# Score tiles of a windowed attention grouped by key tile instead of query tile, in a fused attention and gMLP kernel

## The chip, the cores and the metric

The kernel runs on one core of one Trainium2 chip. The metric is device time in microseconds (us) of one launch, as the median of several runs.

## The reference

Four batches, eight heads, 768 positions, head size 64. Attention keeps the first 4 keys (sinks) and the last 128 positions (the window); a gated MLP with a mixing matrix over positions follows.

```python
scores = q @ k.T / sqrt(64)
keep = (key < 4) | ((0 <= query - key) & (query - key < 128))
a = softmax(where(keep, scores, -1e9))
x = (a @ v) with the heads side by side            # 4 x 768 x 512
h = gelu_tanh(x @ w_in)                            # 512 -> 1024
u, v = h[..., :512], h[..., 512:]
v_n = (v - mean(v)) / sqrt(var(v) + 1e-6) * g_ln
v_s = w_sg @ v_n + b_sg                            # mixes the 768 positions
out = x + (u * v_s) @ w_out
```

## The kernel before, in words

Positions are cut into six tiles of 128. With a window of 128 a query tile i needs only two key tiles, i (the causal triangle) and i-1 (the other triangle), and the four sinks. Heads are taken in pairs p = 0 to 3: the two heads of a pair lie in the lower and the upper 64 rows, so their score matmuls use one half of TensorE's rows each.

The whole kernel is one list of steps, STEPS, written out by hand. The program walks it once, and each engine gets its instructions in that order, one queue for each engine. A step is a name, indices and sometimes a letter for the engine (D VectorE, A ScalarE, P GpSimd). Nothing is reordered afterwards: an instruction that waits holds back all that stands behind it on its engine. The steps that matter here, with batch b, pair p and group g:

- LQ.b.t, LK.b.t (line 223) load one 128-position tile of q or k in bf16. They are issued by GpSimd and share one queue with the loads of v (LVH) and of the weights (LW, LWS, LWO).
- TQ.b.g, TK.b.g transpose two tiles, 2g and 2g+1, of q or k on TensorE (line 377) into a slot of the mm ring; EQ.b.g and EK.b.g copy the result out (lines 197, 198). In batch 0 a step takes a pair of heads and all six tiles (line 371). In batch 3 DQ.3.g and DK.3.g do it by DMA on SyncE's queue (SP) instead.
- QK.b.p.g (lines 473 and 478) makes the score tile of group g, for both heads of the pair, in a slot of the sc ring. In some steps of batch 0 a mask is added first by a matmul with the identity (line 473).
- EX.b.p.g (line 483) is the exponential into a tile P[b, p, g]; MK.b.p.g masks it, by a multiplication on VectorE (line 490) or by two selects on GpSimd (lines 493 and 496).
- SK.b.g (line 457) and SX.b.g (line 462) make the scores of the sinks and their exponential.
- AV.b.p.k (lines 519, 523 and 526) multiplies with v: for each query tile the diagonal part, the part of the previous key tile, and the sinks. In batch 0 one step makes two query tiles, in the others three. NR.b.p.k divides by the sum (lines 535 and 536) into x_sb.
- XT, XE or XD.b.h (a DMA transpose on SP) transpose x_sb into xT; MV (line 561) and GV (line 565), MU (line 602) and GU (line 607) are the first matmul and the Gelu; BN, RS, NM and Z the normalization; SP.b.h.dc (line 622) the mixing matmul, GT (line 627) and GM (line 632) the gate; OU.b.t (line 639), RA.b.t (line 643) and ST.b.t the last matmul, the addition and the store. (The step SP has nothing to do with the engine SP.)
- Steps of one batch are interleaved with those of the next: the attention of batch 1 and 2 runs beside the MLP of the batch before it.

Memory is held in rings: a step that makes a tile takes the next slot and has to wait until all readers of the tile that was there are done. The sc ring has 2 slots, the mm ring 4 (shared by TQ, TK, SK, AV, XT, SP, OU), the P ring 10.

A score tile of group g in the kernel before has 512 columns for each head (384 for g=0), grouped by the two query tiles 2g and 2g+1: key 2g with queries 2g and 2g+1 in columns 0 to 255, key 2g+1 with query 2g+1 in 256 to 383, and, for g>0, key 2g-1 with query 2g in 384 to 511.

Of the kernel before, what the change touches and what calls it, by code (L numbers as in the profile page):

```python
# [28 lines left out]
XE.0.1.A LK.1.2 NR.0.0.2 MK.0.3.2.D LK.1.3 NR.0.1.2 AV.0.2.2 AV.0.3.2 LQ.1.2 NR.0.2.2 GV.0.0 MV.0.1 NR.0.3.2 LQ.1.3  # L29
BN.0.0 LWS.1 XT.0.2 GV.0.1 MU.0.1 XE.0.2.A BN.0.1 WT.0 GU.0.1 TK.1.0 MV.0.2 RS.0.1 EK.1.0.A LK.1.4 NM.0.1 WE.0.A WT.1  # L30
GV.0.2 LK.1.5 TK.1.1 MU.0.2 LB.P EK.1.1.A BN.0.2 Z.0.0.A LK.2.0 WT.2 GU.0.2 MU.0.0 WE.1.D RS.0.2 WE.2.D Z.0.1.A LQ.2.0
NM.0.2 Z.0.2.A Z.0.3.D Z.0.4.D WT.3 LQ.2.1 WT.4 GU.0.0 WE.3.D WT.5 LQ.1.4 Z.0.5.D TQ.1.1 QK.1.0.0 EQ.1.1.D QK.1.1.0
LQ.1.5 SP.0.0.0 WE.4.D LK.2.1 EX.1.0.0 VSM.1 SP.0.0.1 WE.5.D EX.1.1.0 LVH.1.0 GT.0.0.0 TK.1.2 KS.1 GT.0.0.1 QK.1.2.0
QK.1.3.0 EX.1.2.0 SP.0.0.2 LVH.1.1 GM.0.0.0.D EX.1.3.0 MK.1.2.0.D TQ.2.0 EK.1.2.A LQ.2.2 QK.1.0.1 EQ.2.0.D QK.1.1.1
TQ.1.2 EX.1.0.1 GT.0.0.2 LWO SP.0.0.3 EQ.1.2.D EX.1.1.1 LK.2.2 MK.1.0.1.D TK.2.0 MK.1.0.0.D QK.1.2.1 LK.2.3 EK.2.0.A
QK.1.3.1 MK.1.3.0.D SK.1.0 GM.0.0.1.D LQ.2.3 SP.0.1.0 EX.1.2.1 GT.0.0.3 MK.1.1.0.D LQ.2.4 EX.1.3.1 SP.0.1.1 MK.1.1.1.D
LQ.2.5 MK.1.2.1.D SX.1.0 QK.1.0.2 QK.1.1.2 GT.0.1.0 EX.1.0.2 GM.0.0.2.P SP.0.1.2 GT.0.1.1 EX.1.1.2 LK.2.4 GM.0.1.0.D
AV.1.0.0 MK.1.3.1.D AV.1.1.0 LK.2.5 GM.0.0.3.D QK.1.2.2 GT.0.1.2 QK.1.3.2 EX.1.2.2 SP.0.1.3 NR.1.0.0 MK.1.1.2.P
EX.1.3.2 NR.1.1.0 AV.1.2.0 AV.1.3.0 MK.1.0.2.P GT.0.1.3 QK.2.0.0 QK.2.1.0 NR.1.2.0 EX.2.0.0 OU.0.0 MK.1.2.2.P NR.1.3.0
TK.2.1 RA.0.0 AV.1.0.1 XD.1.0 EK.2.1.A MK.1.3.2.P AV.1.1.1 NR.1.0.1 AV.1.2.1 EX.2.1.0 GM.0.1.2.P NR.1.1.1 AV.1.3.1  # L40
NR.1.2.1 QK.2.2.0 LK.3.0 QK.2.3.0 EX.2.2.0 OU.0.1 NR.1.3.1 GM.0.1.3.P EX.2.3.0 OU.0.2 XD.1.1 RA.0.1 GM.0.1.1.P TK.2.2
MK.2.3.0.D TQ.2.1 LVH.2.0 TQ.2.2 EQ.2.1.D MV.1.0 EQ.2.2.D LQ.3.0 EK.2.2.D LQ.3.1 VSM.2 MU.1.0 GV.1.0 MK.2.1.0.D
# [33 lines left out]
def kernel(  # L76
# [14 lines left out]
    nc = tc.nc  # L91
# [9 lines left out]
    NT = S // 128  # L101
# [326 lines left out]
    def at(ring, b):  # L428
        if HOW[b] in "AGL":
            return ring[b].rearrange("p (c t i) -> p t c i", c=HP, t=NT)  # L430
        return ring[b].rearrange("p (t c i) -> p t c i", c=HP, t=NT)
# [31 lines left out]
                             func=AF.Exp, scale=scale)  # L463

    def wide(g):
        return 512 if g else 384

    def QK(b, p, g, biased=0):
        sc = fresh(sc_ring, (b, p, g))
        w = wide(g)  # L470
        if biased:
            for hl in range(2):
                nc.tensor.matmul(sc[:, hl, 0:w], iden, (bias1 if g else bias0)[:, 0:w], start=True, stop=False)
        pieces = [(2 * g, 2 * g, 2, 0), (2 * g + 1, 2 * g + 1, 1, 256)] + ([(2 * g - 1, 2 * g, 1, 384)] if g else [])
        for n, (j, i, ni, c) in enumerate(pieces):
            for hl in range(2):
                rows = slice(64 * hl, 64 * hl + 64)
                nc.tensor.matmul(sc[:, hl, c:c + 128 * ni], at(kT, b)[rows, j, p, :], at(qT, b)[rows, i:i + ni, p, :],  # L478
                                 start=not biased, stop=(not biased or n == len(pieces) - 1))

    def EX(b, p, g):
        w = wide(g)
        nc.scalar.activation(out=P.new((b, p, g))[:, :, 0:w], in_=sc_ring[b, p, g][:, :, 0:w], func=AF.Exp, scale=scale)  # L483

    def MK(b, p, g, e="D"):
        w = wide(g)
        pt = P[b, p, g]
        if e == "D":
            m = (mask1 if g else mask0)[:, 0:w]
            nc.vector.tensor_mul(pt[:, :, 0:w], pt[:, :, 0:w], m.unsqueeze(1).to_broadcast([128, 2, w]))  # L490
            return
        p4 = pt.rearrange("p h (j i) -> p h j i", i=256)
        nc.gpsimd.affine_select(out=p4[:, :, :, 0:128], in_=p4[:, :, :, 0:128], compare_op=ALU.is_ge,  # L493
                                fill=0.0, base=0, pattern=[[0, 2], [0, 2], [1, 128]],
                                channel_multiplier=-1)
        nc.gpsimd.affine_select(out=p4[:, :, :, 128:256], in_=p4[:, :, :, 128:256],
                                compare_op=ALU.is_ge, fill=0.0, base=-1,
                                pattern=[[0, 2], [0, 2], [-1, 128]], channel_multiplier=1)

    def rowsof(b, k):  # L500
        return (2 * k, 2) if b in PARTS else (3 * k, 3)

    def av_view(b, p, k):
        n = rowsof(b, k)[1]
        return mm_ring["a", b, p, k][:, 0:2 * n * (Dh + 1)].rearrange("p (i h d) -> p i h d", i=n, h=2)

    def AV(b, p, k):
        vb = v_sb[b]
        fresh(mm_ring, ("a", b, p, k))
        av = av_view(b, p, k)  # L510
        i0, n = rowsof(b, k)
        first = True
        for il in range(n):
            i = i0 + il
            for hl in range(2):
                h = 2 * p + hl
                pt = P[b, p, i // 2]
                c = 256 * (i % 2)
                nc.tensor.matmul(av[:, il, hl, :], pt[:, hl, c:c + 128], vb[:, h, i, :], start=first, stop=False)  # L519
# [191 lines left out]
```

## Time and profile before

| | |
|---|---|
| median of 3 runs | 156.57 us (156.06 to 156.64) |
| profiled execution: span, first to last instruction | 155.8 us |
| TensorE matmul, busy | 147.2 us (94%), 1543 instructions |
| VectorE, busy | 123.0 us (79%) |
| GpSimd, busy | 99.7 us (64%) |
| ScalarE, busy | 98.9 us (63%) |
| score matmuls, line 478 | 256 instructions |
| software DMA queue (loads issued by GpSimd) | 64608 packets, 11.01 MB, 97.1% of 16 engines' span |

The profile is of one execution, with its own span of 155.8 us; no other time of that execution is given, and the median of the runs is 0.77 us above the span. In the profile PE is TensorE's matmuls, PEld its weight loads, DVE is VectorE, ACT ScalarE, POOL GpSimd, SP SyncE. A row of a group gives line, engine and operation, what is written and read, the count, the busy time and the mean of one in ns, and the idle time of the engine ahead of it with what ended it. A row of the chain or of the timeline begins with the start and the duration in us. A row of a stretch gives its length, the busy time and count of PE, PEld, DVE, ACT and POOL, the granted TensorE clock (1.00 is full), and the DMA share and rate.

### The profile page before, as it was taken

What the parts mean: (1) busy time and instruction counts of PE and PEld (TensorE: products, weight loads), DVE (VectorE), ACT (ScalarE), POOL (GpSimd) and SP (SyncE); (2) the same over time, 40 slices, a digit from 0 to 9 for tenths busy, and PEclk for the clock granted to TensorE, in tenths of its full rate; (3) what the DMA queues carried; (4) which work ended last, traced back from release to release, by engine and by line L of the source; (5) the groups of instructions that cost most, each with busy time, mean ns of one, the idle gap of its engine ahead of it and who ended that gap; (6) DMA issues with size and microseconds to landing.
All of it is one profiled execution on the core that took longest, in us unless ns stands there. A gap on an engine that the chain in (4) does not pass through costs nothing.

```text
span 155.8 us, 3844 instructions
## 1 busy us (share of the span) xinstructions
PE 147.2 (94%) x1543; PEld 95.0 (61%) x1543; DVE 123.0 (79%) x295; ACT 98.9 (63%) x110; POOL 99.7 (64%) x127
## 2 busy tenths in 40 slices
PE   6998799999999999989999999999999999999990
PEld 2455487779775776747566764486567644876530
DVE  4576688829989989769789887899689956867981
ACT  3689789799989856276897855269954025591000
POOL 4099669578999899999559869640798610300400
PEclk9999689999999999999999999999999999999999
DMA  5899999999999999999999299995710580510064
GB/s 162 277 369 155 152 194 163 170 186 200 141 144 145 188 157 169 148 152 156 155 227 235 68 279 177 181 192 47 248 72 6 99 236 0 202 64 9 0 230 176
DMA packets 86170, 24.67 MB, mean 158 GB/s; under 512 B 78660, under 2 KB 83016, under 8 KB 86152
## 3 DMA queue, kind: packets, MB, share of 16 engines
q0 software_dynamic: 64608, 11.01, 97.1%
q1 hardware_dynamic: 21544, 13.41, 32.1%
q8 instruction: 12, 0.20, 0.5%
q14 instruction: 6, 0.05, 0.1%
HBM read 24.81 MB, written 6.29 MB: 200 GB/s over the span
## 4 chain that ended last, share of the span: by engine, by line
PE 75%; DMA 15%; DVE 2%; POOL 2%; issue 1%; ACT 1%; SPq 1%; ACTq 0%
PE mm L622 17%; PE sc L561 13%; PE mm L639 13%; PE sc L602 12%; DMA k<-in_k_dram 6%; DMA v_sb<-in_v_dram 6%; PE sc L478 5%; PE mm L519 4%; DMA uT<-in_k_dram 4%; PE mm L377 3%; PE mm L523 3%; PE mm L526 2%; PE mm L614 1%; PE mm L545 1%; DVE P L490 1%
## 5 line engine op out<-in xcount | busy, mean ns | idle before, releaser
L483 ACT ACTIVATE P<-sc 128x1024 bf16<-128x1024 f32 (+1 forms) x48 | 43.5, 956 | 10.9 <-PE sc L478 10.8
L622 PE MATMUL mm<-wsgT,z 128*128 128x384 bf16 x192 | 34.1, 327 | 0.0
L622 PEld LDWEIGHTS <-z 128*128 128x128 bf16 x192 | 17.7, 98 | 11.9 <-issue 0.7
L561 PE MATMUL sc<-w_in_sb,xT 128*128 128x512 bf16 x96 | 22.2, 379 | 0.7 <-ACT vt L565 0.7
L639 PE MATMUL mm<-w_out_sb,wsg_gated 128*128 128x512 bf16 x96 | 22.7, 379 | 0.0
L493 POOL TENSOR_SCALAR_AFFINE_SELECT P<-P 128x512 bf16<-128x512 bf16 x21 | 14.0, 665 | 13.3 <-ACT P L483 13.0
L627 DVE SCALAR_TENSOR_TENSOR gtmp<-mm,g_sb,b_bc 128x384 bf16<-128x384 f32 x32 | 19.1, 610 | 4.2 <-PE mm L622 3.6
L602 PE MATMUL sc<-xT,w_in_sb 128*128 128x256 bf16 x192 | 22.1, 273 | 0.0
L632 POOL TENSOR_TENSOR wsg_gated<-gtmp,uT 128x384 bf16<-128x384 bf16 x15 | 14.9, 1005 | 10.9 <-DVE gtmp L627 10.9
L574 DVE BATCH_NORM_STATS2 st<-vt 128x6 f32<-128x512 f32 x24 | 15.4, 684 | 7.5 <-ACT vt L565 7.4
L602 PEld LDWEIGHTS <-w_in_sb 128*128 128x128 bf16 x192 | 18.7, 98 | 3.0
L536 DVE TENSOR_TENSOR x_sb<-mm,rcp 128x384 bf16<-128x384 f32 (+1 forms) x36 | 18.5, 513 | 1.2
L565 ACT ACTIVATE vt<-sc 128x1024 f32<-128x1024 f32 x12 | 12.3, 1027 | 9.0 <-PE sc L561 8.9
L519 PE MATMUL mm<-v_sb,P 128*128 128x65 bf16 x192 | 16.8, 198 | 1.0 <-DMA v_sb<-in_v_dram 0.9
L643 DVE TENSOR_TENSOR ot<-mm,x_sb 128x512 f32<-128x512 f32 x24 | 16.1, 683 | 2.0 <-PE mm L639 1.9
L583 POOL TENSOR_TENSOR rs<-rs,neg_half 128x4 f32<-128x4 f32 (+1 forms) x8 | 7.0, 869 | 16.4 <-DVE rs L578 15.0
L519 PEld LDWEIGHTS <-P 128*128 128x128 bf16 x192 | 15.1, 100 | 2.9 <-issue 1.5
L223 POOL DMA_DIRECT2D q<-in_q_dram x18 | 16.7, 949 | 0.0
L223 POOL DMA_DIRECT2D k<-in_k_dram x18 | 16.4, 924 | 0.5 <-POOL wsg_gated L632 0.5
L523 PE MATMUL mm<-v_sb,P 128*128 128x65 bf16 x160 | 16.1, 197 | 0.0
L561 PEld LDWEIGHTS <-xT 128*128 128x128 bf16 x96 | 9.2, 98 | 10.9 <-issue 0.9
L478 PE MATMUL sc<-qT,kT 64*128 64x128 bf16 (+1 forms) x256 | 15.1, 242 | 0.6 <-ACT P L483 0.3
(90 smaller groups left out, 238.0 us busy)
## 6 DMA issues: line engine op xcount, KB each, us to landing
out_dram<-ot SPq DMA_DIRECT2D x24, 256.0 KB, 2.3
v_sb<-in_v_dram POOLq DMA_DIRECT2D x8, 384.0 KB, 8.5
q<-in_q_dram POOLq DMA_DIRECT2D x18, 128.0 KB, 6.3
k<-in_k_dram POOLq DMA_DIRECT2D x18, 128.0 KB, 6.5
wsg_gated<-in_moe_w_sg_dram POOLq DMA_DIRECT2D x2, 576.0 KB, 7.5
w_in_sb<-in_moe_w_in_dram POOLq DMA_DIRECT2D x2, 512.0 KB, 10.1
uT<-in_q_dram SPq DMA_DIRECT2D x2, 384.0 KB, 3.1
uT<-in_k_dram SPq DMA_DIRECT2D x2, 384.0 KB
```

The costliest lines, as they stand in the source:

```text
L223: return nc.gpsimd.dma_start(out=dst.rearrange("p (h d) -> p h d", h=H), in_=heads(src, b, i))
L478: nc.tensor.matmul(sc[:, hl, c:c + 128 * ni], at(kT, b)[rows, j, p, :], at(qT, b)[rows, i:i + ni, p, :], start=not biased, stop=(not biase ...
L483: nc.scalar.activation(out=P.new((b, p, g))[:, :, 0:w], in_=sc_ring[b, p, g][:, :, 0:w], func=AF.Exp, scale=scale)
L519: nc.tensor.matmul(av[:, il, hl, :], pt[:, hl, c:c + 128], vb[:, h, i, :], start=first, stop=False)
L523: nc.tensor.matmul(av[:, il, hl, :], pt[:, hl, c:c + 128], vb[:, h, i - 1, :], start=False, stop=(i < 2 and il == n - 1 and hl == 1))
L536: nc.vector.tensor_mul(x_sb.get(b)[:, i0:i0 + n, 128 * p:128 * (p + 1)].rearrange("p t (h d) -> p t h d", h=2), av[:, :, :, 0:Dh], rcp[:, ...
L561: nc.tensor.matmul(hp[:, jl, :], xT[b][:, 2 * g + jl, c, :], w_in_sb[:, c, d_half:2 * d_half], start=(c == 0), stop=(c == KD - 1))
L602: nc.tensor.matmul(hp[:, dc // 2, 256 * (dc % 2):256 * (dc % 2 + 1)], w_in_sb[:, c, 128 * dc:128 * (dc + 1)], xT[b][:, 2 * g:2 * g + 2, c, :],
L622: nc.tensor.matmul(ps[:, 0:NH], z[b][:, si, 128 * dc:128 * (dc + 1)], wsgT[:, si, NH * hf:NH * (hf + 1)], start=(si == 0), stop=(si == NT ...
L627: nc.vector.scalar_tensor_tensor(out=gtmp.new((b, hf, dc)), in0=mm_ring["g", b, hf, dc][:, 0:NH], scalar=g_sb[:, dc:dc + 1], in1=b_bc[:, N ...
L639: nc.tensor.matmul(ps, gated(b, hf)[:, dc, 128 * tl:128 * (tl + 1)], w_out_sb[:, dc, :], start=(dc == 0), stop=(dc == KU - 1))
L643: nc.vector.tensor_add(ot.new((b, t)), mm_ring["o", b, t], x_sb[b][:, t, :])
```

## The change

The score tiles are grouped by key tile. The tile of group g now holds key 2g with queries 2g and 2g+1, and key 2g+1 with queries 2g+1 and 2g+2, 256 columns each; the last group (g=2) has only query 5 for key 5, so it is the one with 384 columns. A step has two matmuls per head instead of three (g=0 had two already). AV takes the part of the previous key tile from the tile of the group that this key belongs to. The second select on GpSimd covers one block per head instead of two in the last group.

Since QK.b.p.g now reads query tile 2g+2, some steps move: EQ.1.1 ahead of QK.1.0.0 (which now stands behind SP.0.0.0), TQ.1.2 and EQ.1.2 ahead of QK.1.0.1 in exchange for TQ.2.0 and EQ.2.0, and TQ.2.1 and EQ.2.1 from behind TK.2.2 to behind SP.0.1.3 and NR.1.0.0, ahead of QK.2.0.0. The loads keep their order. In STEPS, lines 32 to 42 change (only moved steps and their neighbours are shown, the line breaks are not):

```diff
-... TQ.1.1 QK.1.0.0 EQ.1.1.D QK.1.1.0 LQ.1.5 SP.0.0.0 WE.4.D ...
+... TQ.1.1 EQ.1.1.D LQ.1.5 SP.0.0.0 QK.1.0.0 QK.1.1.0 WE.4.D ...
-... MK.1.2.0.D TQ.2.0 EK.1.2.A LQ.2.2 QK.1.0.1 EQ.2.0.D QK.1.1.1 TQ.1.2 EX.1.0.1 GT.0.0.2 LWO SP.0.0.3 EQ.1.2.D EX.1.1.1 ...
+... MK.1.2.0.D TQ.1.2 EK.1.2.A LQ.2.2 EQ.1.2.D QK.1.0.1 QK.1.1.1 TQ.2.0 EX.1.0.1 GT.0.0.2 LWO SP.0.0.3 EQ.2.0.D EX.1.1.1 ...
-... SP.0.1.3 NR.1.0.0 MK.1.1.2.P EX.1.3.2 NR.1.1.0 AV.1.2.0 AV.1.3.0 MK.1.0.2.P GT.0.1.3 QK.2.0.0 QK.2.1.0 NR.1.2.0 ...
+... SP.0.1.3 TQ.2.1 NR.1.0.0 MK.1.1.2.P EX.1.3.2 EQ.2.1.D NR.1.1.0 AV.1.2.0 AV.1.3.0 MK.1.0.2.P GT.0.1.3 QK.2.0.0 QK.2.1.0 NR.1.2.0 ...
-... TK.2.2 MK.2.3.0.D TQ.2.1 LVH.2.0 TQ.2.2 EQ.2.1.D MV.1.0 EQ.2.2.D ...
+... TK.2.2 MK.2.3.0.D LVH.2.0 TQ.2.2 MV.1.0 EQ.2.2.D ...
```

```diff
     def wide(g):
-        return 512 if g else 384
+        return 384 if g == NT // 2 - 1 else 512
...
-        pieces = [(2 * g, 2 * g, 2, 0), (2 * g + 1, 2 * g + 1, 1, 256)] + ([(2 * g - 1, 2 * g, 1, 384)] if g else [])
-        for n, (j, i, ni, c) in enumerate(pieces):
+        pieces = [(2 * g, 2, 0), (2 * g + 1, min(2, NT - 2 * g - 1), 256)]
+        for n, (j, ni, c) in enumerate(pieces):
             for hl in range(2):
                 rows = slice(64 * hl, 64 * hl + 64)
-                nc.tensor.matmul(sc[:, hl, c:c + 128 * ni], at(kT, b)[rows, j, p, :], at(qT, b)[rows, i:i + ni, p, :],
+                nc.tensor.matmul(sc[:, hl, c:c + 128 * ni], at(kT, b)[rows, j, p, :], at(qT, b)[rows, j:j + ni, p, :],
...
-        nc.gpsimd.affine_select(out=p4[:, :, :, 128:256], in_=p4[:, :, :, 128:256],
+        n = w // 128 - 2
+        nc.gpsimd.affine_select(out=p4[:, :, 0:n, 128:256], in_=p4[:, :, 0:n, 128:256],
                                 compare_op=ALU.is_ge, fill=0.0, base=-1,
-                                pattern=[[0, 2], [0, 2], [-1, 128]], channel_multiplier=1)
+                                pattern=[[0, 2], [0, n], [-1, 128]], channel_multiplier=1)
...
                 if i >= 1:
-                    c = 128 if i % 2 else 384
-                    nc.tensor.matmul(av[:, il, hl, :], pt[:, hl, c:c + 128], vb[:, h, i - 1, :],
+                    c = 256 * ((i - 1) % 2) + 128
+                    nc.tensor.matmul(av[:, il, hl, :], P[b, p, (i - 1) // 2][:, hl, c:c + 128], vb[:, h, i - 1, :],
                                      start=False, stop=(i < 2 and il == n - 1 and hl == 1))
```

More of the change, by code (lines that the diff above doesn't have):

```diff
@@ L31 @@
 GV.0.2 LK.1.5 TK.1.1 MU.0.2 LB.P EK.1.1.A BN.0.2 Z.0.0.A LK.2.0 WT.2 GU.0.2 MU.0.0 WE.1.D RS.0.2 WE.2.D Z.0.1.A LQ.2.0
[L32 to L35, printed above, removed]
+NM.0.2 Z.0.2.A Z.0.3.D Z.0.4.D WT.3 LQ.2.1 WT.4 GU.0.0 WE.3.D WT.5 LQ.1.4 Z.0.5.D TQ.1.1 EQ.1.1.D LQ.1.5 SP.0.0.0
@@ L36 @@
+QK.1.0.0 QK.1.1.0 WE.4.D LK.2.1 EX.1.0.0 VSM.1 SP.0.0.1 WE.5.D EX.1.1.0 LVH.1.0 GT.0.0.0 TK.1.2 KS.1 GT.0.0.1 QK.1.2.0
+QK.1.3.0 EX.1.2.0 SP.0.0.2 LVH.1.1 GM.0.0.0.D EX.1.3.0 MK.1.2.0.D TQ.1.2 EK.1.2.A LQ.2.2 EQ.1.2.D QK.1.0.1 QK.1.1.1
+TQ.2.0 EX.1.0.1 GT.0.0.2 LWO SP.0.0.3 EQ.2.0.D EX.1.1.1 LK.2.2 MK.1.0.1.D TK.2.0 MK.1.0.0.D QK.1.2.1 LK.2.3 EK.2.0.A
 QK.1.3.1 MK.1.3.0.D SK.1.0 GM.0.0.1.D LQ.2.3 SP.0.1.0 EX.1.2.1 GT.0.0.3 MK.1.1.0.D LQ.2.4 EX.1.3.1 SP.0.1.1 MK.1.1.1.D
 LQ.2.5 MK.1.2.1.D SX.1.0 QK.1.0.2 QK.1.1.2 GT.0.1.0 EX.1.0.2 GM.0.0.2.P SP.0.1.2 GT.0.1.1 EX.1.1.2 LK.2.4 GM.0.1.0.D
-AV.1.0.0 MK.1.3.1.D AV.1.1.0 LK.2.5 GM.0.0.3.D QK.1.2.2 GT.0.1.2 QK.1.3.2 EX.1.2.2 SP.0.1.3 NR.1.0.0 MK.1.1.2.P
@@ L39 @@
[L39 to L42, printed above, removed]
+AV.1.0.0 MK.1.3.1.D AV.1.1.0 LK.2.5 GM.0.0.3.D QK.1.2.2 GT.0.1.2 QK.1.3.2 EX.1.2.2 SP.0.1.3 TQ.2.1 NR.1.0.0 MK.1.1.2.P
@@ L43 @@
+EX.1.3.2 EQ.2.1.D NR.1.1.0 AV.1.2.0 AV.1.3.0 MK.1.0.2.P GT.0.1.3 QK.2.0.0 QK.2.1.0 NR.1.2.0 EX.2.0.0 OU.0.0 MK.1.2.2.P
+NR.1.3.0 TK.2.1 RA.0.0 AV.1.0.1 XD.1.0 EK.2.1.A MK.1.3.2.P AV.1.1.1 NR.1.0.1 AV.1.2.1 EX.2.1.0 GM.0.1.2.P NR.1.1.1
+AV.1.3.1 NR.1.2.1 QK.2.2.0 LK.3.0 QK.2.3.0 EX.2.2.0 OU.0.1 NR.1.3.1 GM.0.1.3.P EX.2.3.0 OU.0.2 XD.1.1 RA.0.1
+GM.0.1.1.P TK.2.2 MK.2.3.0.D LVH.2.0 TQ.2.2 MV.1.0 EQ.2.2.D LQ.3.0 EK.2.2.D LQ.3.1 VSM.2 MU.1.0 GV.1.0 MK.2.1.0.D
 LVH.2.1 BN.1.0 MV.1.1 GU.1.0 LQ.3.2 RA.0.2 LQ.3.3 MK.2.0.0.D MV.1.2 GV.1.1 MK.2.2.0.D LK.3.1 KS.2 LK.3.2 BN.1.1 MU.1.1
```

## The prediction

> **What bounds the kernel now.** I read the page first, then the chain of waits, then the timeline around the one place where a step is moved far.
>
> ```profile
> PE 147.2 (94%) x1543; PEld 95.0 (61%) x1543; DVE 123.0 (79%) x295; ACT 98.9 (63%) x110; POOL 99.7 (64%) x127
> ```
>
> ```profile
> PE 75%; DMA 15%; DVE 2%; POOL 2%; issue 1%; ACT 1%; SPq 1%; ACTq 0%
> ```
>
> TensorE (PE) carries the end. It runs one queue in the order that STEPS gives, so only two things move the time: how long PE's own work takes, and where PE, in its order, meets something that isn't there yet. The score matmuls (line 478) stand in the chain in blocks of two QK steps:
>
> ```profile
> 40.16 0.44 PE sc L478 x8
> ...
> 71.20 3.49 PE sc L602 x32
> ...
> 80.50 0.55 PE sc L478 x12
> ```
>
> The first block is two steps with g=0 (each one pair of 256-column and one pair of 128-column matmuls, the two heads in the two row halves, starting some 3 ns apart), the last is two steps with g>0 (one 256 pair, two 128 pairs each). The two more pairs cost 0.55-0.44=0.11 us, so a 128 pair costs 0.055. Line 602 gives 3.49/32=0.109 for 256 columns. What is left of the first block, 0.44-2x(0.109+0.055)=0.11, belongs to the block (in the starts of the matmuls, about 0.1 lost on entering and 0.1 on leaving, part of it in the neighbours), not to a matmul.
>
> The other reading is of what PE waits for. Between the start (until 17.15 us, when the first half of v lands) and the end there is hardly a wait on a DMA but this:
>
> ```profile
> 46.81 0.81 POOL k L223
> 47.62 9.45 DMA k<-in_k_dram
> 57.07 0.05 issue
> 57.12 0.40 PE mm L377 x4
> ```
>
> This is LK.2.3, needed by the second half of TK.2.1. It left GpSimd at 47.62 and landed 9.45 later; PE lost 0.43 us for it. The queue serves in order and is full: issues run far ahead of the landings. LQ.2.3 is the next issue behind it:
>
> ```profile
> 48.48 2.72 POOL L223 DMA_DIRECT2D q<-in_q_dram  x3
> ```
>
> ```profile
> DMA to landing us min/median/max: 4.2/6.3/9.4
> ```
>
> The second line is for the q tile: LQ.2.3 is its slowest load, 48.48+9.35=57.83, which the landing marks of the trace show too (LK.2.3 57.07, LQ.2.3 57.83, LQ.2.4 58.7).
>
> **The change, part by part.**
>
> *Fewer matmuls.* Each (batch, pair of heads) goes from 16 to 12 score matmuls, 256 to 192 in all; the columns stay (1408 a head). A pair of 128s on one key tile, until now split over two steps, becomes one pair of 256: 2x0.055 becomes 0.109. There are 2x16=32 such mergers, about 0.001 to 0.003 us each: -0.1 us at most. The rows of the profile suggest more:
>
> ```profile
> L478 PE MATMUL sc<-qT,kT 64*128 64x256 bf16 x96 | 12.2, 280 | 0.6 <-ACT P L483 0.3 <-DVE qT L198 0.2 <-ACT kT L197 0.2
> L478 PE MATMUL sc<-qT,kT 64*128 64x128 bf16 x160 | 11.6, 219 | 0.0
> ```
>
> 11.6/160=0.073 us a matmul would make 64x0.073=4.7 us; but busy time there overlaps, and the block arithmetic shows that columns are paid, not instructions. Between -4.7 and 0 I take -0.1, by the blocks.
>
> *Bias.* Line 473 gets 384 instead of 512 columns in QK.0.0.2.1 and 512 instead of 384 in QK.0.3.0.1: zero.
>
> *Exponentials (line 483).* g=0 grows from 768 to 1024 elements (814 to 1027 ns), g=2 shrinks by the same, 16 each: zero in sum. The growth in batch 0 (three by 17 us, 0.64 us) lies in front of the wait for v until 17.15 and of the score slots that PE reaches later still. If that cover failed, it would be up to 0.6.
>
> *Masks.* On VectorE 15 multiplications grow and 3 shrink: net 12x(0.14 to 0.27) us, +1.7 to +3.3 busy (0.54 against 0.68 alone; 549 against 823 in the mean). On GpSimd 12 of the second selects halve: 12x0.3=-3.8 busy. Before 58 us the wait below swallows the VectorE part; behind it, it falls where VectorE idles (7.4 us in total for the Gelu before its statistics). One place pays back: MK.2.2.2.D, in the chain at 88.47 with 1.08 us, shrinks, and the 0.22 us for which PE waits there goes: -0.2.
>
> *EX.0.3.2* now waits for AV.0.0.2 (it overwrites P[0,0,1], which AV.0.0.2 newly reads). AV.0.0.2 ends about 24.5, EX.0.3.2 began at 23.88: 0.6 later, 0.2 given back by its own shortness. Behind it on ScalarE are XE.0.1.A and the table load of GV.0.0; PE's next use of that score slot is MV.0.1 at 27.5. Zero, with 2 us of cover.
>
> *TQ.1.2/EQ.1.2.D ahead of QK.1.0.1, TQ.2.0 behind.* TQ.1.2 comes at 44.45 where TQ.2.0 was; its last tile LQ.1.5 lands at 45.1, and QK.1.0.1 then waits for the copy EQ.1.2.D (0.69). PE leaves this place about 1.2 us later. SP.0.0.0 ahead of QK.1.0.0 covers EQ.1.1.D and costs nothing.
>
> *TQ.2.1/EQ.2.1.D* move from behind TK.2.2 to behind SP.0.1.3, since QK.2.0.0 now reads query tile 2. On PE, AV.1.2.0 is queued behind it:
>
> ```profile
> 53.35 1.15 PE L622 MATMUL mm<-wsgT,z 128*128 128x384 bf16 x6
> 54.34 0.26 PE L519 MATMUL mm<-v_sb,P 128*128 128x65 bf16 x3
> ```
>
> So PE reaches it at 54.34, or 55.6 with the 1.2 above, does the half of tile 2 and stands until 57.83 for LQ.2.3. All earlier delay, up to 2.2 us, vanishes in this wait. On VectorE EQ.2.1.D stands between these:
>
> ```profile
> 53.90 0.56 DVE L536 TENSOR_TENSOR x_sb<-mm,rcp 128x384 bf16<-128x384 f32 x1
> 54.37 0.18 DVE L535 RECIPROCAL rcp<-mm 128x6 f32<-128x6 f32 x1
> 54.59 0.56 DVE L536 TENSOR_TENSOR x_sb<-mm,rcp 128x384 bf16<-128x384 f32 x1
> 55.07 0.61 DVE L627 SCALAR_TENSOR_TENSOR gtmp<-mm,g_sb,b_bc 128x384 bf16<-128x384 f32 x1
> ```
>
> that is, behind NR.1.0.0 and ahead of NR.1.1.0, GT.0.1.3, NR.1.2.0, NR.1.3.0, which all wait with it. And TQ.2.1 takes a slot of the four-deep mm ring, so AV.1.3.0 gets the slot of AV.1.1.0 (before: of AV.1.0.0) and must wait for NR.1.1.0. The working: PE goes on at 57.88; the copy starts 0.43 later (as EK.2.1.A, 57.12 to 57.55), at 58.31; NR.1.1.0 starts 0.61 later (45.10 to 45.71 for EQ.2.0.D and its follower), its product ends 0.77 after that: 59.69. AV.1.2.0 is done at 58.47, so PE stands another 1.25. Then AV.1.3.0 0.36, QK.2.0.0 and QK.2.1.0 with their block 0.64, OU.0.0 0.86, TK.2.1 0.45: AV.1.0.1 begins at 62.05, where it began at 57.35: +4.7, less 0.45 for TQ.2.1, which is no longer done later: +4.25. The 0.43 wait of TK.2.1 is gone in this sum. XD.1.0, behind NR.1.3.0 on SP's queue, issues at about 61.6 and lands by 66.5 (slowest transpose 4.9), MV.1.0 comes at 67.5: hidden by 1 us, and paid one for one beyond that. From there on PE is dense and nothing else is tied to an absolute time, the loads being early now; nothing absorbs it.
>
> *Sum.* 4.25-0.2-0.05 (the mergers behind 58 us)=+4.0 on the span of 155.8: 159.8. The median of the runs is 0.77 above that span, so 156.57+4.0=160.6.
>
> **The clock.**
>
> ```profile
> 13.71:17.12 3.41, 1.87 (x47) 1.31 (x42) 3.33 (x7) 3.41 (x6) 3.00 (x4) 1.00 3.39 138
> 17.12:20.54 3.42, 3.39 (x43) 2.44 (x43) 1.49 (x7) 2.32 (x5) 1.23 (x2) 0.50 2.27 176
> ```
>
> PE's granted clock (the column before the last two) fell to 0.50 for 3.41 us behind a stretch in which PE was busy 1.87 us and no gap was over 1.1 us. The new stall leaves some 1.5 us of work in 54.67:58.08. That speaks for the first rival below. The Trainium skill (TensorE: Matmul & The Clock Gate, Part 1: The HAM clock gate) ties the half clock to at least one idle window of about 3.4 us; by that rule a stall of 2.2 us costs no clock and the sum stays as it is. This trace disagrees: its fall came without an idle window.
>
> **Rivals.** (1) *The clock falls as well.* For: the row above. Against: 150.24:153.66 was busy only 1.43, and the clock's records show no fall before 157. AV.1.3.0, the two QK and part of OU.0.0 at half clock: 0.36+0.44+0.2=+1.0, 161.6. (2) *The wait in VectorE doesn't reach PE*, the stall is the landing alone: +4.0-1.25, 159.3. Against it stands the ring order. (3) *Not slower*: LQ.2.3 lands before PE comes to it. The point is 55.6; it would have to land 2.2 us earlier, and LK.2.3 with it. Then 156.57-0.43-0.2-0.1=155.8. Against it: the queue is full from 17 to 61 us and the bytes are the same. Were each dropped matmul worth its 0.073 us, some of its 4.7 could show only behind the stall, 32 matmuls, 2.3: still +1.7, 158.2.
>
> **Numbers.** Forecast (160.6) 0.5, rival 1 0.3, rival 2 0.1, matmuls paid 0.04, rival 3 0.06. The range 159.0 to 162.0 takes in the first three. Faster or slower than 0.5% is what a measurement of this kernel can tell from no change. Rival 3 sits at that edge, so faster 0.03, same 0.03, slower 0.94.
>
> **What would show it.** Right: a wait of the form PE mm L377 on a q load of about 2.2 us near 55.6 to 57.9, a VectorE wait for PE before a qT copy, a wait of AV.1.3.0 for x_sb, score blocks of 0.55, 0.55, 0.44. Wrong: no such wait, or a PE that catches up behind 62 us, or a half clock at 58 (rival 1).

## The result and the profile after

The change makes the kernel slower by more than forecast: 167.14 us median (165.86 to 167.31, four runs) against 156.60 of the kernel before beside it, a ratio of 1.064 (95% interval 1.060 to 1.069). The forecast was 160.6, its range ended at 162.0. The profiled execution of after took 167.3 us with a span of 165.6; before's span was 155.8. So 9.8 us of span have to be explained, and the working had found 4.0. A few of the kernels below ran in two groups of times; the ratios leave the disturbed runs out, and where the groups matter they are given. Line numbers move by one or two from kernel to kernel, and a row of dots marks what a view or a diff leaves out.

The page of after, its first line of busy times and the shares of the chain:

```profile
PE 148.2 (89%) x1479; PEld 91.9 (56%) x1479; DVE 125.7 (76%) x295; ACT 99.1 (60%) x110; POOL 97.8 (59%) x127
...
PEclk9999999999999999995799999999999999999999
...
PE 62%; DMA 22%; POOL 7%; DVE 2%; issue 2%; ACT 2%; SPq 1%
```

The 64 matmuls are gone (1543 to 1479), but PE's share of the chain fell from 75% to 62% and that of DMA rose from 15% to 22%. PE waits, and the clock falls once, in the slices at 75 to 83 us.

The chain of waits of after, around the place that was forecast and the one that was not:

```profile
47.50 9.23 DMA q<-in_q_dram
56.73 0.05 issue
56.78 0.41 PE mm L377 x4
57.21 0.69 DVE qT L198
57.91 0.11 DVE rcp L536
58.04 0.57 DVE x_sb L537
58.61 0.04 issue
58.65 0.25 PE mm L520 x3
...
59.17 0.54 PE sc L478 x8
...
63.82 0.79 PE mm L640 x4
64.61 12.32 DMA xT<-x_sb
76.93 0.05 issue
76.98 4.55 PE sc L562 x12
```

The first eight rows are the forecast wait, link by link: LQ.2.3 lands, the second half of TQ.2.1, its copy EQ.2.1.D, then NR.1.1.0 (reciprocal and product), and only then AV.1.3.0. The block of 0.54 is QK.2.0.0 and QK.2.1.0 in their new form. The row of 12.32 us was not forecast: XD.1.1, the DMA transpose of the second half of batch 1's x_sb, for which MV.1.1 waits.

The transposes of that line, before and after, from the view of the line. It issues six; the last row covers the two whose landing the view tells, XD.1.1 (4.95 before, 12.32 after) and XD.2.0 (3.7 before, 5.4 after):

```profile
DMA to landing us min/median/max: 3.7/4.3/4.9
```

```profile
L553 SPq DMA_TRANSPOSE xT<-x_sb x6: 1310/1596/3272, 60.5 to 133.9; - x6
...
who waited for it (us, times):
  PEld L562: 6.0, 2
  PE sc L562: 5.2, 1
...
DMA to landing us min/median/max: 5.4/8.8/12.3
```

Before, nobody waited for one, and XD.1.1 took 4.9. What stands beside it is seen in GpSimd's timeline, before first, then after:

```profile
60.08 0.94 POOL L223 DMA_DIRECT2D k<-in_k_dram  x1
61.04 2.12 POOL L632 TENSOR_TENSOR wsg_gated<-gtmp,uT 128x384 bf16<-128x384 bf16 x2
63.11 1.47 POOL L269 DMA_DIRECT2D v_sb<-in_v_dram  x1
```

```profile
59.20 0.94 POOL L223 DMA_DIRECT2D k<-in_k_dram  x1
60.16 1.80 POOL L633 TENSOR_TENSOR wsg_gated<-gtmp,uT 128x384 bf16<-128x384 bf16 x2
61.89 1.47 POOL L269 DMA_DIRECT2D v_sb<-in_v_dram  x1
63.36 1.76 POOL L223 DMA_DIRECT2D q<-in_q_dram  x2
65.09 1.44 POOL L269 DMA_DIRECT2D v_sb<-in_v_dram  x1
```

The load at 63.11 and 61.89 is LVH.2.0, the first of a row of nine. It isn't held by anything on PE. Before, XD.1.1 was issued at 60.98, 2.1 us ahead of it. After, PE and with it XD.1.1 came 3.6 us later (64.61), while GpSimd came 1.2 us earlier: the transpose now stands 2.7 us behind the loads. Of the 1.2 us GpSimd had 0.6 already at the issue of LK.2.4 (52.07 instead of 52.65); its eight selects won 0.3 and the three products behind them 0.3. The 3.6 us of PE alone would have put XD.1.1 1.5 us behind.

Last, the busy time by stretches of the clock (columns as in the section on the profile before; the granted clock is the number ahead of the last two):

```profile
70.38:73.80 3.42, 1.02 (x4) 0.29 (x3) 3.09 (x7) 1.21 (x2) 0.88 (x1) 1.00 2.11 110
73.80:77.21 3.41, 0.23 (x1) 0.13 (x2) 0.29 (x2) 0.00 (x0) 0.00 (x0) 0.50 3.95 135
77.21:80.63 3.42, 3.42 (x9) 1.21 (x8) 0.61 (x1) 1.02 (x1) 0.00 (x0) 0.50 2.36 150
```

The clock is at 0.50 from 73.80 to 80.63. The first 3.2 us of that are idle anyway; after the landing nine matmuls of 512 columns (line 562) take about 0.43 us each instead of 0.216, so 1.9 us.

The starts of PE's steps give the account, after minus before:

| step | before | after | later by |
|---|---|---|---|
| MV.1.0 | 63.24 | 66.39 | 3.15 |
| MV.1.1 | 67.58 | 70.73 | 3.15 |
| MV.1.2 | 69.31 | 78.66 | 9.35 |
| MU.1.2 | 72.78 | 83.11 | 10.33 |
| MV.2.0 | 93.32 | 103.24 | 9.92 |
| OU.3.5, the last | 150.64 | 160.35 | 9.71 |

3.15 is the forecast place, 7.2 more arise between MV.1.1 and MU.1.2 (5.2 of waiting for the landing, 1.9 of clock, by the rows above), and 0.6 come back later.

### The profile page after: what moved, and what is told of

The parts are those of the page before. It is cut to its first block, busy times and chain, and to the rows that moved or that the text cites. A ratio compares the mean times of both kernels' runs of the same rounds, so it can differ in the third digit from the quotient of the medians.

```text
span 165.6 us, 3716 instructions
## 1 busy us (share of the span) xinstructions
PE 148.2 (89%) x1479; PEld 91.9 (56%) x1479; DVE 125.7 (76%) x295; ACT 99.1 (60%) x110; POOL 97.8 (59%) x127
## 4 chain that ended last, share of the span: by engine, by line
PE 62%; DMA 22%; POOL 7%; DVE 2%; issue 2%; ACT 2%; SPq 1%
PE mm L623 15%; PE mm L640 12%; PE sc L562 11%; PE sc L603 9%; DMA xT<-x_sb 7%; DMA q<-in_q_dram 6%; DMA v_sb<-in_v_dram 5%; PE sc L478 4%; DMA uT<-in_k_dram 4%; PE mm L520 3%; PE mm L524 3%; POOL q L223 2%; POOL v_sb L269 2%; PE mm L527 2%; PE mm L377 1%
## 5 line engine op out<-in xcount | busy, mean ns | idle before, releaser
L562 PE MATMUL sc<-w_in_sb,xT 128*128 128x512 bf16 x96 | 24.2, 401 | 5.9 <-DMA xT<-x_sb 5.2
L566 ACT ACTIVATE vt<-sc 128x1024 f32<-128x1024 f32 x12 | 12.3, 1024 | 15.9 <-PE sc L562 15.8
L493 POOL TENSOR_SCALAR_AFFINE_SELECT P<-P 128x512 bf16<-128x512 bf16 x21 | 14.5, 690 | 11.6 <-ACT P L483 11.4
L520 PE MATMUL mm<-v_sb,P 128*128 128x65 bf16 x192 | 15.9, 194 | 1.5 <-DVE x_sb L537 1.1
L490 DVE TENSOR_TENSOR P<-P,mask 128x1024 bf16<-128x1024 bf16 (+1 forms) x23 | 16.5, 738 | 1.0 <-ACT P L483 0.8
L520 PEld LDWEIGHTS <-P 128*128 128x128 bf16 x192 | 14.6, 97 | 3.7 <-issue 2.7
L478 PE MATMUL sc<-qT,kT 64*128 64x256 bf16 x192 | 15.0, 263 | 1.4 <-DVE qT L198 1.0
```

The source lines that it names most:

```text
L562: nc.tensor.matmul(hp[:, jl, :], xT[b][:, 2 * g + jl, c, :], w_in_sb[:, c, d_half:2 * d_half], start=(c == 0), stop=(c == KD - 1))
```

## The experiments

The theory that they test: what was not forecast is one mechanism, the DMA transpose XD.1.1 standing behind the queued loads, and the clock on top. Rivals: the regrouped tiles cost it themselves; the clock is the main part; or the wait at TQ.2.1 costs all of it through something else.

**The moves without the regrouping.** Before's code with after's list of steps.

> The kernel before with the changed order of steps alone, score tiles still grouped by query tile (three matmuls a head). Theory (the moved TQ.2.1 stands in TensorE's queue until LQ.2.3 lands, XD.1.1 goes out late, behind the loads LVH.2.0 to LK.3.3, and MV.1.1 waits for it): as slow as the changed kernel, 166 to 168 us, with a wait of MV.1.1 for xT of 4 to 6 us. Rival (the regrouping itself costs: larger first tiles, longer masks, the new wait of EX.0.3.2): under 159 us.

Measured: 166.42 us (165.87 to 168.0), ratio 1.061 (1.054 to 1.069). In its trace AV.1.3.0 waits 1.28 us, XD.1.1 is issued at 66.2, 5.0 behind LVH.2.0, and lands 9.7 later. MV.1.1 waits 2.7 us for it, less than the 4 to 6 expected, but the clock also fell from 56.74 to 63.57, which it didn't in the profiled run of after. So the two totals agree by partly different ways. The new tiles are not needed for either stall: the order of the steps alone costs all but some 0.7 us, which the intervals don't tell from nothing.

**The late move taken back.** After, with TQ.2.1 behind AV.1.1.1 and TK.2.1, and what needs it later:

```diff
-... SP.0.1.3 TQ.2.1 NR.1.0.0 ... EX.1.3.2 EQ.2.1.D NR.1.1.0 ... GT.0.1.3 QK.2.0.0 QK.2.1.0 NR.1.2.0 ...
+... SP.0.1.3 NR.1.0.0 ... EX.1.3.2 NR.1.1.0 ... GT.0.1.3 NR.1.2.0 ... AV.1.0.1 ... AV.1.1.1 TK.2.1 NR.1.0.1 EK.2.1.A TQ.2.1 GM.0.1.2.P EQ.2.1.A AV.1.2.1 ... NR.1.2.1 QK.2.0.0 LK.3.0 QK.2.1.0 ...
```

> The changed kernel, but TQ.2.1 stands behind TK.2.1 (its copy on ScalarE), and QK.2.0.0 to QK.2.3.0 and their exponentials behind AV.1.3.1, so that nothing in TensorE's queue waits for LQ.2.3; the steps around TQ.1.2 stay as in the change. Theory: the wait at 55 to 58 us is gone, XD.1.1 goes out ahead of LVH.2.0, MV.1.1 no longer waits: 156 to 158 us. Rival (regrouping costs): over 160 us.

Measured: 158.17 us, just above the theory's 156 to 158, ratio 1.0065 (1.0029 to 1.0102). Seven of ten runs took 157.1 to 158.9, three 160.9 to 163.5. In the profiled run (span 157.1, clock 1.00 to the end) XD.1.1 goes at 61.75, 0.97 ahead of LVH.2.0, lands 6.1 later, and nobody waits. So both stalls hang on the place of TQ.2.1 and of the score steps that follow it. Of what is still slower the trace shows a wait of 0.74 us at QK.1.0.1; that the rest follows from it is not shown.

**The loads held back until the transpose has landed.** After, with LVH.2.0 made to wait for XD.1.1:

```diff
-HOLDS = ""
+HOLDS = "LVH.2.0<XD.1.1"
```

> The changed kernel, with one wait more: LVH.2.0 (and so all loads behind it on GpSimd) is issued after XD.1.1 has landed. Theory: XD.1.1 lands within 5 us of its issue instead of 12.3, MV.1.1 waits less than 0.5 us, the clock stays at 1.00, and what is left is the wait at TQ.2.1: 159 to 161 us. Rival (XD.1.1 is slow for another reason, as its own issue on SyncE or x_sb being late): still 165 us or more.

Measured: 165.69 us (165.13 to 166.39), ratio 1.055 (1.049 to 1.061). The landing is as the theory has it (within 5 us), and the total isn't (159 to 161). The chain, then GpSimd's and PE's timeline of this kernel:

```profile
66.11 3.94 DMA xT<-x_sb
```

```profile
70.61 1.47 POOL L269 DMA_DIRECT2D v_sb<-in_v_dram  x1 [8.90 <-DMA xT<-x_sb]
...
76.94 2.68 POOL L223 DMA_DIRECT2D k<-in_k_dram  x3
79.56 1.11 POOL L584 TENSOR_TENSOR rs<-rs,neg_half 128x4 f32<-128x4 f32 x1
```

```profile
82.72 0.49 PE L478 MATMUL sc<-qT,kT 64*128 64x256 bf16 x4 [1.87 <-ACT uT L608]
```

Alone, the transpose takes 3.94 us instead of 12.32, and MV.1.1 no longer waits for it. But the nine issues now stand ahead of RS.1.1 (line 584) on GpSimd, which delays the normalization, and PE waits 1.87 us for the Gelu behind it. The clock fell twice here (59.0 to 62.4 and 82.9 to 86.3). The wait was moved, not removed.

**The same, with four loads moved behind RS.1.2**, to keep GpSimd free:

```diff
-... LK.3.1 KS.2 LK.3.2 BN.1.1 ... LK.3.3 BN.1.2 RS.1.1 MU.1.2 GU.1.1 LQ.3.4 ... RS.1.2 OU.0.3 ...
+... KS.2 BN.1.1 ... BN.1.2 RS.1.1 MU.1.2 GU.1.1 ... RS.1.2 LK.3.1 LK.3.2 LK.3.3 LQ.3.4 OU.0.3 ...
```

> As the run with the loads behind XD.1.1, but LK.3.1 to LK.3.3 and LQ.3.4 stand behind RS.1.2 on GpSimd, so that RS.1.1 no longer waits for their issue. Theory: XD.1.1 lands within 5 us, and without the wait for RS.1.1 (2.0 us at 80.6, and the fall of the clock after it) what is left is the wait at TQ.2.1 and the half clock that follows it: 160 to 162.5 us. Rival (the loads, delayed, are missed elsewhere): over 164 us.

Measured: 162.62, 164.85, 165.32 and 166.15 us; ratio 1.043 (1.032 to 1.054). The profiled run is the first. In it the clock stays at 1.00, XD.1.1 lands after 4.2 us, MV.1.2 begins at 72.29, 2.98 later than before, which is the forecast's part and no more. Then the late loads meet batch 3's own transposes: DK.3.0 lands 7.3 us after its issue instead of 4.6, KS.3 on VectorE waits for it, and PE waits 1.8 us behind VectorE. VectorE's timeline, then PE's:

```profile
89.31 0.19 DVE L444 TENSOR_TENSOR ks_sink<-kT,halfsel 128x32 bf16<-128x32 bf16 x1 [2.99 <-DMA kT<-k]
```

```profile
90.78 0.25 PE L519 MATMUL mm<-v_sb,P 128*128 128x65 bf16 x3 [1.76 <-DVE gtmp L627]
```

The timed median lies where the rival had it; the trace of the one run is the theory's. The other three runs have granted clocks of 0.979 to 0.986, against 1.00 in the profiled one, so falls of the clock belong to their difference.

**The loads too early in the kernel before.** Before, with nothing changed but LVH.2.0 and LVH.2.1 issued ahead of LK.3.0:

```diff
-... LK.3.0 ... LVH.2.0 TQ.2.2 ... LVH.2.1 BN.1.0 ...
+... LVH.2.0 LVH.2.1 LK.3.0 ... TQ.2.2 ... BN.1.0 ...
```

> The kernel before, in which only LVH.2.0 and LVH.2.1 are issued earlier, ahead of LK.3.0 on GpSimd, so that they are in the queue when XD.1.1 goes out at 61 us; nothing is regrouped and no TensorE step moves. Theory (a DMA transpose that meets queued loads lands late): XD.1.1 takes over 7 us instead of 5, MV.1.1 waits for it, 158 to 163 us. Rival (the loads do not hold up a transpose; in the changed kernel it was late by itself): within 1 us of before.

Measured: 161.66 us (160.39 to 162.33), ratio 1.029 (1.023 to 1.036). Chain and PE's timeline:

```profile
61.56 9.33 DMA xT<-x_sb
```

```profile
70.94 4.45 PE L560 MATMUL sc<-w_in_sb,xT 128*128 128x512 bf16 x12 [1.80 <-DMA xT<-x_sb]
```

This is the cleanest of the runs: the transpose is issued 0.6 us later than in before, PE runs 0.5 us later, and 0.96 us behind LVH.2.0 instead of 2.1 ahead it takes 9.3 us instead of 4.95. The clock fell at 71.07 as well. The mechanism needs nothing of the change under study.

**The clock kept up.** After, with 20 matmuls without use (HM.20) ahead of MV.1.1, so that PE is busy while it waits.

> The changed kernel with 20 matmuls on zeros ahead of MV.1.1 (4.3 us of TensorE, inside its wait for XD.1.1 of 5.2 us; their output is overwritten). Theory: the half clock from 73.8 to 80.6 us comes of the idle wait and costs 9 matmuls x 0.21 = 1.9 us; kept busy, the clock stays at 1.00 and the time is 165.0 to 165.6 us. Rival (the clock falls for another reason, or its fall is hidden by another wait): no change, 167 us, or more by what of the 4.3 us isn't hidden.

Measured: 166.08 us (165.02 to 167.71), ratio 1.052 (1.044 to 1.061). XD.1.1 lands at 76.8 as in after (76.93), the clock is 1.00 from 62.4 on, and MU.1.2 begins at 81.9 instead of 83.1. So by these two traces 1.2 us, of the 1.9 that the matmuls lost, can be had this way, and the clock isn't the main part. The intervals of the two ratios overlap, so the timed runs alone don't show the gain; the theory's 165.0 to 165.6 us was a little too low. This run had its one fall at 59.0 instead.

**The copy on ScalarE.** After, with `EQ.2.1.A` for `EQ.2.1.D`, which takes NR.1.1.0 out of the copy's shadow.

> The changed kernel with the copy EQ.2.1 on ScalarE instead of VectorE, at the same place in the order. VectorE then no longer waits for TQ.2.1, and NR.1.1.0 frees the mm slot of AV.1.3.0 early. Theory: the wait of AV.1.3.0 (1.28 us) goes, but XD.1.1 still goes out behind LVH.2.0, so MV.1.1 still waits until some 76 us: no more than 1.5 us faster than the changed kernel, 165 to 167 us. Rival (VectorE held back is what makes the rest late): under 162 us.

Measured: 164.58 us (163.52 to 165.51), ratio 1.048 (1.040 to 1.056). That is 2.6 us below after, where the theory had 1.5 at most. AV.1.3.0 follows AV.1.2.0 at once (57.39 behind 57.02), 0.34 us of waiting appears at QK.2.0.0 instead, and MV.1.0 comes 0.92 earlier. XD.1.1 still goes 1.9 behind LVH.2.0 and takes 10.9: the second stall stays, with a fall of the clock for one stretch (74.76 to 78.18) where after has two.

**What a matmul is worth.** Before, with each score matmul of 256 columns split in two of 128 (352 matmuls instead of 256):

```diff
+        pieces = [(j, i + x, 1, c + 128 * x) for j, i, ni, c in pieces for x in range(ni)]
```

> The kernel before, with each 256-column score matmul split into two of 128 columns: 96 score matmuls more (352), the same columns. Theory (columns are paid, 0.055 us a pair of 128, not instructions): within 0.4 us of before. Rival (an instruction costs its 0.073 us of the busy row): 96 x 0.073 = 7 us slower.

Measured: 157.33 us (ten runs, 156.58 to 158.99), ratio 1.0036 (0.9997 to 1.0075). 96 matmuls more cost 0.6 us, not told from nothing, where 0.073 each would be 7.0. Columns are paid. The profiled run (span 156.95, 1.15 above that of before) shows where its excess lies, and it isn't in the score matmuls. From its chain and PE's timeline:

```profile
56.28 8.02 DMA xT<-x_sb
```

```profile
64.34 1.90 PE L562 MATMUL sc<-w_in_sb,xT 128*128 128x512 bf16 x8 [1.09 <-DMA xT<-x_sb]
```

This is XD.1.0, issued behind six loads that had not landed yet; MV.1.0 waits 1.1 us for it.

**Both moves made late.** The kernel of the second experiment, with TQ.2.0 and TQ.1.2 earlier and more work between the copy EQ.1.2.D and QK.1.0.1. And the same list with before's tiles.

> The regrouped kernel with TQ.2.1 late as in the run before of that kind, and around TQ.1.2 the order TQ.2.0, TQ.1.2, SP.0.0.3, QK.1.0.1, QK.1.1.1 (EK.1.2 ahead of EX.1.2.0), so that TensorE has SP.0.0.3 to do while LQ.1.5 lands and EQ.1.2 copies. Theory: the 0.74 us wait at QK.1.0.1 goes and the kernel comes to within 0.6 us of before, 156.2 to 157.4 us. Rival (that wait is swallowed by a later one on a load, as a load's landing is fixed): 158 us, as with TQ.2.1 late alone.

> The very order of steps of the other run of this call, with the score tiles grouped by query tile as before (three matmuls a head). The difference of the two is the regrouping by itself. Theory: 0.1 us for 64 matmuls less, and masks that cost VectorE more and GpSimd less, both beside TensorE: the two within 0.5 us. Rival (64 matmuls fewer are worth their busy rows, 4.7 us, or the larger first tiles cost): over 1.5 us apart, either way.

Measured: the first gave 157.96 and 158.54, then 161.66 to 163.16 in four runs; the second 160.07 and 160.67, then 166.97 to 169.6 in four. Both miss what was expected. The pair is 2.1 us apart in the shorter runs and about 5 in the longer ones, with the old tiles slower, so the condition of the rival (over 1.5) is met. But the moves alone were no slower than after, and the runs of both kernels fall into two groups, so this is no price of the tiles. In the profiled run of the first, one of its long ones, XD.1.1 goes 1.08 behind LVH.2.0 and lands 10.2 later, and PE waits 1.9 us for it. In that of the second, one of its short ones, it goes 0.44 behind and lands 8.6 later, and PE waits 0.4. So standing behind the loads doesn't by itself make a run long, and what parts the groups stays open.

**GpSimd a little later.** The kernel of the second experiment again, to make its race safe: first with GM.0.1.0 moved from VectorE to GpSimd ahead of LVH.2.0, then instead with GM.0.1.1 done twice there.

> The kernel of e2 with the gate multiplication GM.0.1.0 moved from VectorE (before AV.1.0.0) to GpSimd, behind GM.0.1.1 and so ahead of LVH.2.0. It is there only to put about 0.9 us of work on GpSimd between the issue of XD.1.1 and that of LVH.2.0. In e2's profile XD.1.1 went at 61.76, 0.97 ahead of LVH.2.0 (62.73), and landed 6.1 later; three of e2's ten runs took 160.9 to 163.5 us where the others took 157.1 to 158.9. Theory (who is issued first decides, and the slow runs are those in which the loads went first or nearly so): XD.1.1 goes 1.7 to 2.0 us ahead, lands 4.5 to 5.5 after its issue, and the runs of 160.9 and more are gone or at most one in ten; median 157.0 to 158.0. Rival (the slow runs come from the clock or from the loads' own order, whatever XD.1.1 does): two to four of ten runs stay above 160.5, median 157.5 to 159. Second rival (later loads cost what they save): all runs about 0.9 us longer, 158.5 to 159.5, since LK.3, LQ.3 and LVH.2.1 are all 0.9 later.

Measured: 158.58 us median, but seven of thirteen runs took 156.9 to 158.6 and six 163.8 to 169.8. The theory is out: the long runs became more, not fewer. The median is the first rival's, the share of long runs above its two to four in ten. The profiled run is one of the long ones (165.17). VectorE's timeline, then PE's:

```profile
54.02 0.67 DVE L489 TENSOR_TENSOR P<-P,mask 128x1024 bf16<-128x1024 bf16 x1
54.61 3.94 DVE L632 TENSOR_TENSOR wsg_gated<-gtmp,uT 128x384 bf16<-128x384 bf16 x1
58.48 0.60 DVE L627 SCALAR_TENSOR_TENSOR gtmp<-mm,g_sb,b_bc 128x384 bf16<-128x384 f32 x1
```

```profile
59.13 0.25 PE L519 MATMUL mm<-v_sb,P 128*128 128x65 bf16 x3 [3.47 <-DMA k<-in_k_dram]
```

A product that took 0.35 us in the second experiment took 3.94, while GpSimd made eight selects without a gap from 54.79 to 58.83. The releaser that PE's row names is not it, its landings were over: AV.1.2.0 needs a slot of the mm ring, whose reader GT.0.1.2 (the row at 58.48) stood behind that product. So PE came late to XD.1.1, and this run doesn't test the theory. That the move had shifted VectorE against GpSimd is argued, not shown.

> The kernel of e2 with the gate multiplication GM.0.1.1 done twice on GpSimd, one behind the other, ahead of LVH.2.0: 0.9 us more on GpSimd there and nothing changed on VectorE (e11 also took a product off VectorE, and there the next product of VectorE, GM.0.0.3, took 3.94 us beside GpSimd's selects where 0.35 is usual, which held PE for 3.5 us before the place in question). Theory (who is issued first decides): XD.1.1 goes 1.7 to 2.0 us ahead of LVH.2.0 and lands 4.5 to 5.5 after its issue, so runs of 160.5 us and more become rarer than e2's three in ten, at most one or two of ten; median 157.0 to 158.3. Rival 1 (the long runs are the same VectorE product beside GpSimd's selects, or the clock, and have nothing to do with XD.1.1): three or more of ten runs stay above 160.5. Rival 2 (the later loads cost what the landing saves): all runs about 0.9 longer, median 159.

Measured: 159.78 us (158.5 to 162.14, six runs), ratio 1.0153 (1.0107 to 1.0199). One run of six is over 160.5. In the profiled run XD.1.1 is issued at 63.36, only 0.29 ahead of LVH.2.0, and lands 3.8 later, the least in the view of its line:

```profile
DMA to landing us min/median/max: 3.8/4.6/5.4
```

The landing is better than the theory's; the distance (1.7 to 2.0 expected) and the median (157.0 to 158.3) miss it, since XD.1.1 comes 1.6 us later than in the second experiment. By the trace that product took 0.79 here and the mask ahead of it 0.90 instead of 0.68, and PE waited 0.99 us behind them. The second rival is not seen: from MU.1.2 to OU.3.5 this run takes 77.7 us, before 77.9, so the later loads cost nothing there.

All profiled runs together, one execution of each kernel:

| kernel | XD.1.1 issued, against LVH.2.0 | us to its landing |
|---|---|---|
| loads held back (two kernels) | 4.5 and 4.7 ahead | 3.9, 4.2 |
| before | 2.1 ahead | 4.95 |
| score matmuls split | 1.3 ahead | 6.5 |
| late TQ.2.1 | 0.97 ahead | 6.1 |
| the same, GM.0.1.1 twice | 0.29 ahead | 3.8 |
| both late, old tiles | 0.44 behind | 8.6 |
| before, loads early | 0.96 behind | 9.3 |
| both late | 1.08 behind | 10.2 |
| copy on ScalarE | 1.9 behind | 10.9 |
| after | 2.7 behind | 12.3 |
| late TQ.2.1, GM.0.1.0 moved | 3.0 behind | 9.8 |
| clock kept up | 4.2 behind | 10.5 |
| moves only | 5.0 behind | 9.7 |

Ahead, it takes 3.8 to 6.5 us; behind, 8.6 to 12.3; there is nothing between. For the order of issue that is shown over fourteen kernels.

## Why the prediction was right and wrong

*Right: the stall at TQ.2.1.* The wait for LQ.2.3, the copy's place on VectorE, the ring slot and AV.1.3.0's wait came as written. AV.1.3.0 stood 1.28 us (forecast 1.25). MV.1.0 came 3.15 later, not 4.25: LQ.2.3 landed at 56.73 and not at 57.83, the queue of loads running 1.1 us earlier in this execution, and that is the whole difference. The wait at TQ.1.2 did vanish in it. That PE reached TQ.2.1 at 55.75, as forecast (55.6), is partly luck: 0.81 us of it was a wait for the slot of the mm ring that GT.0.1.2 on VectorE still read, which the working did not have, and the wait for the load swallowed it. Rival 2 fell with AV.1.3.0's wait, rival 3 with the order of PE reaching TQ.2.1 (55.75) and the landing (56.73).

*Right: the prices of matmuls, masks and blocks.* Score blocks of 0.54, 0.55 and 0.43 to 0.44 us stand in the chain. The groups of after show what busy time is worth:

```profile
L478 PE MATMUL sc<-qT,kT 64*128 64x256 bf16 x160 | 14.4, 273 | 1.4 <-DVE qT L198 1.0 <-DVE kT L198 0.3 <-ACT kT L197 0.2
...
L478 PE MATMUL sc<-qT,kT 64*128 64x128 bf16 x32 | 3.2, 216 | 0.0
```

That is 17.6 us busy against 23.8 before: 6.2 us less, and none of it seen in the time. The masks on VectorE grew by 1.9 us (forecast 1.7 to 3.3), GpSimd's selects fell by 2.1 (forecast 3.8, since the others took a little longer), and 0.23 came back between AV.2.0.0 and MV.2.0, where the shorter mask was forecast to give back 0.2. Two slips of the working change nothing: its parts behind 59.69 add up to 62.00, not 62.05, and the paid matmuls to 158.3, not 158.2.

*Wrong: one sentence of the sum.* It read that XD.1.0 "lands by 66.5 (slowest transpose 4.9)", and that "from there on PE is dense and nothing else is tied to an absolute time, the loads being early now". Three faults are in it. XD.1.1, the second transpose, was not followed at all, though MV.1.1 waits for it. The price of 4.9 was XD.1.1's own, from an issue 2.1 us ahead of the loads, and the delay that was being added up moved it behind them; it was not the slowest either, for the view covers two transposes, and XD.1.0 of before landed 5.7 us after its issue by its landing marks in the trace. And the loads being early was not the harmless part but the cause: LVH.2.0 hangs on GpSimd alone, so every us that PE lost moved it ahead of XD.1.1. The 1.2 us by which GpSimd was early added to it, but only 0.3 of that came of the selects; with the old selects, in the moves alone, LVH.2.0 went out earlier still (61.24). The order could be read from before's trace: 2.1 us of distance against a forecast delay of 4.25. The price of the wrong order could not: the one transpose of before that is issued largely while GpSimd issues loads, DK.3.1, goes out 0.46 us ahead of them and lands in 4.4.

The missed term: 5.2 us of waiting and 1.9 us of clock. That the first is the order of issue is shown by the loads held back (3.94 and 4.2 us), by the loads made early in the kernel before (9.3) and by the table. That the second is the clock is seen in the trace of the kernel that kept it up, for 1.2 of the 1.9.

What the order acts through is only partly seen. Loads that are queued already lengthen a transpose too, though less. XD.1.0 was issued while GpSimd made selects and landed, by its landing marks, 5.7 us later in before (five loads still to land), 6.4 with the loads early (six) and 8.0 with the score matmuls split (six). The last two transposes of batch 3, with no load in the queue, took 3.6 to 3.7 in every kernel. In the long landings of XD.1.1 the whole issue of the transpose on SyncE lies beside GpSimd's issues of loads; in the short ones 1.4 us of it at most, or nothing. That goes with the order and may be no more than it; SyncE's instruction itself is often longer beside them (3272 ns in the line's view above, 1.5 us before). In after the data packets of XD.1.1 ran, by the trace's packet records, from 68.0 to 74.1 us where before they took 2.6, and the landing mark came 2.8 us behind the last of them, against 0.5. The Trainium skill (DMA: Bandwidth & Descriptors, Queues, rings and completion order) says that each DMA engine takes turns, a packet at a time, between the queues that have work. That fits packets of both kinds side by side; it doesn't tell landings of 5.7 to 8.0 from those of 8.6 to 12.3, and no run here shows what does, beyond the order of issue.

*Rival 1, the clock behind the stall at TQ.2.1.* Not in after's profile; but in those of the moves alone, the loads held back and the clock kept up it fell at 56.7 or 59.0, and MV.1.0 then came at 67.9 to 68.1 instead of 66.2 to 66.4. It is worth 1.7 us, not the 1.0 that was priced, and it differs between executions of nearly the same program. Two other executions of after have a lower mean clock than the profiled one (0.963 and 0.969 against 0.979), so it may have fallen there too. The stretches ahead of the boundary, first after's, then that of the moves alone:

```profile
53.31:56.73 3.42, 2.02 (x21) 1.07 (x18) 3.05 (x7) 1.51 (x2) 3.42 (x6) 1.00 2.40 156
```

```profile
53.33:56.74 3.41, 0.96 (x20) 0.79 (x19) 0.19 (x1) 0.80 (x1) 3.41 (x7) 1.00 2.43 157
```

PE busy 2.02 us, and the clock stays; 0.96, and it falls.

What stays open: whether the three long runs of the second experiment are this race or the VectorE product; what parts the groups of runs of the two kernels with both moves late; and the cost of the regrouping alone, for with one list of steps the new tiles were 0.7 us slower and with another 2 to 5 us faster. No regrouped kernel beats the kernel before (156.6 to 156.9 us beside them); TQ.2.1 made late comes near, 0.3 to 1.0% slower without its three long runs.

## What to carry to other kernels

When a delay is forecast on one engine, list every transfer that is issued behind it and every transfer that isn't, and check whether the two change places; a price for a transfer holds only for the order in which it was measured. An engine that limits nothing still decides when its transfers go out: ask in front of what they go when the others come late. And busy time of overlapping matmuls is no price: 6.2 us less of it were worth nothing here.

## What the runs showed of the hardware

The DMA transpose XD.1.1, issued by SyncE, lands in 3.8 to 6.5 us if it goes before a row of loads from GpSimd's queue, and in 8.6 to 12.3 if it goes behind the first of them. The nearest cases are 0.29 us ahead (3.8) and 0.44 us behind (8.6). A queue of five or six loads issued earlier had a smaller effect on XD.1.0 (5.7, 6.4 and 8.0 us), and with no load queued a transpose of x_sb took 3.6 to 3.7.

The granted clock falls to 0.50 in whole stretches of 3.41 us, behind a stretch with little matmul work, not only behind an idle one. PE's busy time is not the measure: the clock fell behind stretches with 0.17, 0.96, 1.02, 1.16, 1.55 and (in before) 1.87 us busy, and not behind before's with 1.43. The columns of the matmuls order them better. This is an estimate of mine from the traces, at 2.4 columns per ns (512 in 0.216 us) with each ns counted once. Ahead of the falls the stretches hold 0.2 to 1.3 us of columns. Those without a fall behind them hold 1.25 or more, but for two with 1.0 and 1.2 in the kernel with GM.0.1.0 moved, whose trace lacks some matmul records. So a point near a third of the stretch is likely and not shown. The Trainium skill (TensorE: Matmul & The Clock Gate, Part 1: The HAM clock gate) ties the fall to an idle window of about 3.4 us; these rows disagree with it.

A product of two bf16 tiles on VectorE took 3.94 us instead of 0.35 beside a row of GpSimd's selects. The Trainium skill (SBUF — State Buffer, Who interferes with whom) says that a VectorE instruction with two inputs in SBUF contends with a GpSimd instruction that reads SBUF. The trace agrees: the one product lasted from 54.61 to 58.55 us and the row of eight selects from 54.79 to 58.83, so the wait can last over more than one select.
